# Token mixing of batches 2 to 7 written as seven block products instead of eight

## The chip, the cores and the metric

The kernel runs on one core of a Trainium2 chip. The number that counts is the device time of one execution in microseconds (us). The core has engines that run side by side, each working its own instructions strictly in order: TensorE (PE in the profile, matmuls into the PSUM banks), VectorE (DVE), ScalarE (ACT) and GpSimd (POOL). SyncE (SP) issues the transfers, also in order, on one queue. Semaphores tie the engines together, so that an instruction which waits holds up everything behind it on its own engine.

## The reference

```python
# attention: 8 batches, 8 heads, S = 576 positions, head size 64; banded masks
scores = where(mask, q @ k.T / 8, -1e9);  attn = softmax(scores);  o = attn @ v
# mixing: x is o with the heads side by side, 8 x 576 x 512
theta  = x @ w_theta
zr, zi = x * cos(theta), x * sin(theta)
y      = einsum('ts,bsd->btd', w_tok_r, zr) + einsum('ts,bsd->btd', w_tok_i, zi)
u      = x + y
out    = u + max(u @ w_ch, 0)
```

## The kernel before

All matrices are float32. For TensorE each one is split into a high and a low part (type fp32r), and a product is three matmuls: high by high, low by high, high by low. A split costs one ACT instruction (the cast that makes the high part) and one POOL or DVE instruction (the subtraction that makes the low part).

**The token stage** of a batch is the pair of einsums. The function `token` (L836) is called for d = 0 to 3 (128 columns of x) and g = 0, 1 (halves of 288 output positions). Each call sums over nine key tiles: 0 to 3 are 128 rows each of x·cos, 4 to 7 of x·sin, and tile 8 holds the last 64 rows of both. Nine tiles by three matmuls of 128x128 by 128x288 make 27 matmuls a call and 216 a batch (L850), all into one PSUM bank; `residual` (L817) then adds x to the bank on DVE (L825) and splits the sum u on ACT (L828) and POOL (L830). The weights of all 18 blocks (key tile by half) lie in SBUF the whole time: `wtk…`, `late_wt_a`, `late_wt_b`.

**Trig.** `theta` makes x·w_theta in PSUM, one key tile (st) after the other in the order 4, 0, 1, 2, 3. `trig` (L763) makes cosine and sine on ACT (K on L787, then L796, L698, L705) with a DVE step (L789), `by_x` (L745, L748) multiplies each of the two by x on DVE, and `zsplit` (L633) splits each product (ACT L644, POOL L646). Tile 4 begins with a DVE addition (g, L784).

**Attention.** For a pair of heads, `scores` (L441) runs nine small groups of matmuls into two PSUM banks, DVE masks them (L409) and takes the maximum (L498), ACT takes the exponentials (L504), DVE sums and inverts (L507, L508), and POOL multiplies (L510), which gives P. `turn` (L514) transposes P on DVE (L525, eight instructions), `pv` (L603) multiplies by v on TensorE, and x is then evacuated on ACT (L581), split (L593, L597, L599) and turned through DRAM (L729, then transfers).

**Order.** `phase(b, nb)` (L889) writes out the TensorE order by hand for a stage in which batch b is in its token and channel stages while batch nb = b + 1 is in attention and trig. Tables say behind which of the eight token calls the scores and pv of the four pairs stand: `S_AT = {2: 0, 3: 1, 4: 3, 5: 5}` puts pairs 2 and 3 of batch nb and pairs 0 and 1 of batch nb + 1 ahead of calls 0, 1, 3 and 5, `PV_AT` does the same for pv. Behind the eight token calls theta tiles alternate with the first five calls of `chan` (L869, 12 matmuls each, with `finish` on DVE, L859), and three more follow. On the other engines the framework's scheduler sets the order, once, when the program is built.

Of the kernel before, what the change touches and what calls it, by code (L numbers as in the profile page):

```python
# [38 lines left out]
FG0 = {4: ("zl2", "zl6"), 0: ("zl3", "zl7"), 1: ("zh3", "zh7")}  # L39
# [14 lines left out]
NK = 9  # L54

# [96 lines left out]
def build(ctx, tc, qT, kT, vw, wth, wtk, wch, maskb, ident, identb, outT):  # L152
# [17 lines left out]
    def pe(ins):  # L170
        tc.keep_in_program_order(ins)
# [81 lines left out]

    KE = S + 32
# [9 lines left out]
    idt = cp.tile([128, 128], F32, name="idt")  # L264
    mskb = cp.tile([128, 6, BW], BF16, name="mskb")
    idb = cp.tile([128, 128], BF16, name="idb")
# [101 lines left out]
    def token_weights(g, n, stage):  # L368
        cs = slice(HS * g, HS * g + HS)
        c = 2 * n  # L370
        src, sz = (wtk[:, c:c + 2, cs], 2 * HS) if n < 4 else (wtk[:, c, cs], HS)
        T, tag = yield from unpack(src, sz, f"wtk{g}_", stage, g == 0, n, None)
        if g:
            for p in range(NP):
                yield None, ("pv", 0, p)
            t, o = (late("wt_a", 8 * HS), 4 * HS * n) if n < 2 else (late("wt_b", 10 * HS), 4 * HS * (n - 2))
            dst = tuple(t[:, o + i * sz:o + i * sz + sz] for i in range(2))
        else:
# [254 lines left out]
    def zsplit(b, kt, z, rel):  # L633
# [3 lines left out]
        hi = hp.tile([128, DM], F32R, tag=f"zh{kt}", name=f"zh{b}_{kt}")  # L637
        lo = hp.tile([128, DM], F32R, tag=f"zl{kt}", name=f"zl{b}_{kt}")
# [123 lines left out]

    def trig(b, st):  # L763
        cs = slice(128 * st, min(128 * st + 128, S))
# [4 lines left out]
        if b == 0 and st in FG0:  # L769
            K, gt = (hp.tile([128, DM], F32R, tag=t, name=f"{n}{b}_{st}").bitcast(F32) for t, n in zip(FG0[st], "Kg"))  # L770
            K = K.bitcast(I32)[:R]
            rf = rg = None
        else:
            rf, rg = ("f", (yield from take("f", 2))), ("g", (yield from take("g", 2)))
            K = gp.tile([128, DM], I32, tag="f", name=f"K{b}_{st}")[:R]
            gt = gp.tile([128, DM], F32, tag="g", name=f"g{b}_{st}")
# [112 lines left out]
    def phase(b, nb):  # L889
        if nb >= B:  # L890
            for f, i, g in UNITS:
                go(f(b, i, g))
            return
        n = 0
        while n <= TH_AT:
            for p in S_AT:
                if S_AT[p] == n and nb + p // NP < B:
                    go(scores(nb + p // NP, p % NP))
            f, i, g = UNITS[n]
            go(f(b, i, g))  # L900
            for p in range(NP):
                if PV_AT[p] == n:
                    go(pv(nb, p))
            for p in TURN_AT:
                if TURN_AT[p] == n and nb + p // NP < B:
                    go(turn(nb + p // NP, p % NP))
            for p in range(NP):
                if PV_AT[p] == n and nb > 1:
                    x_turn(nb, p)
            if n == STORE_AT and nb > 1:  # L910
                x_store(nb)
            if n == LOAD_AT and nb > 1:
                x_load(nb)
            n += 1
        rest = UNITS[n:]
        for i, st in enumerate(STS):
            go(theta(nb, st))
            f, e, g = rest.pop(0)
            go(f(b, e, g))
            go(trig(nb, st))  # L920
            for p in TURN_TH:
                if TURN_TH[p] == i and nb + p // NP < B:
                    go(turn(nb + p // NP, p % NP))
# [135 lines left out]
```

## Time and profile before

| what | value |
|---|---|
| time, three runs | 578.02, 578.47, 578.80 us; median 578.47 us |
| span of the profiled execution | 576.0 us |
| share of the span busy: PE, DVE, ACT, POOL | 96%, 66%, 60%, 39% |
| instructions: PE, DVE, ACT, POOL | 5464, 1156, 939, 206 |
| read from and written to device memory | 64.49 MB, 16.52 MB |
| packets of the SP queue, as share of 16 engines' span | 43.7% |

The span runs from the first to the last instruction of the profiled execution on the core; the time is the whole execution as the device counts it. The stage of one batch repeats: TensorE starts the scores of pair 2 of the next batch at 273.39, 338.59 and 403.80 us. In the rows of the profile, a busy time is the sum over a group of instructions, "ns" is the mean of one, and the figure behind the bar is the time for which the engine stood idle ahead of the group, with what ended that idle time behind the arrow.

### The profile page before, as it was taken

Reading aid. Unit: us, or ns where it says so; the run is one execution under the profiler, and the core shown is the slowest. Engines: PE = TensorE matmul, PEld = TensorE weight load, DVE = VectorE, ACT = ScalarE, POOL = GpSimd, SP = SyncE. Lnnn points to the kernel's source line nnn. Section 1 sums busy time; section 2 is a strip of 40 time slices with the busy share of each in tenths; the row PEclk is TensorE's granted clock in tenths of the full one; section 3 lists DMA queues with packets and bytes.
Section 4 is the critical chain, followed back from the end, with each engine's and each line's share of the span. In section 5 each row is a group of like instructions: output and inputs, shape, how many; then the busy total and the mean of one; then the engine's idle time right before and its main releaser. Section 6 shows DMA issues by size and latency. Waiting matters only on the chain.

```text
span 576.0 us, 13996 instructions
## 1 busy us (share of the span) xinstructions
PE 550.5 (96%) x5464; PEld 501.6 (87%) x5464; DVE 378.0 (66%) x1156; ACT 345.2 (60%) x939; POOL 222.2 (39%) x206
## 2 busy tenths in 40 slices
PE   5997799999999999999999999999999999999997
PEld 4744688879999899988999899988999899989997
DVE  3879798865666668756776768756775767445112
ACT  1498967768555784369555785359556695266110
POOL 2228855525224352226324253226323353325220
PEclk9999699899999999999999999999999999999999
DMA  8991437601747046540746146550747123321002
GB/s 303 400 368 28 165 105 245 216 0 63 231 150 193 32 162 210 169 127 20 268 143 172 64 148 202 181 136 11 252 146 190 69 83 102 77 89 65 18 1 83
DMA packets 45586, 81.91 MB, mean 142 GB/s; under 512 B 3920, under 2 KB 19024, under 8 KB 45520
## 3 DMA queue, kind: packets, MB, share of 16 engines
q1 hardware_dynamic: 45520, 81.02, 43.7%
q8 instruction: 43, 0.70, 0.5%
q14 instruction: 23, 0.19, 0.1%
HBM read 64.49 MB, written 16.52 MB: 141 GB/s over the span
## 4 chain that ended last, share of the span: by engine, by line
DVE 34%; ACT 30%; PE 25%; issue 5%; POOL 2%; DMA 2%; SPq 0%; ACTq 0%; POOLq 0%; DVEq 0%
DVE pt L525 16%; PE y L850 11%; ACT P L504 11%; PE c L882 6%; PE th L685 3%; DVE P L409 3%; ACT K L698 3%; ACT K L787 3%; DVE xh L599 3%; ACT th L796 2%; ACT zh L644 2%; DVE xq L729 2%; DVE K L789 2%; ACT cos L705 2%; ACT x L581 2%
## 5 line engine op out<-in xcount | busy, mean ns | idle before, releaser
L830 POOL TENSOR_TENSOR u<-x,u 128x288 fp32r<-128x288 f32 x64 | 54.7, 858 | 184.6 <-ACT u L828 184.6
L525 DVE STREAM_TRANSPOSE pt<-P 32x288 f32<-32x288 f32 x224 | 105.1, 469 | 12.0 <-POOL P L510 8.9
L882 PE MATMUL c<-u,late_wc 128*128 128x288 f32 x768 | 110.2, 296 | 2.8 <-DVE x L859 2.8
L882 PEld LDWEIGHTS c<-u,late_wc 128*128 128x128 f32 x768 | 106.0, 188 | 6.8 <-DVE x L859 4.0
L850 PE MATMUL y<-wtkh,zh 128*128 128x288 f32 x288 | 90.3, 314 | 1.1 <-ACT zh L644 1.1
L850 PE MATMUL y<-wtkh,zl 128*128 128x288 f32 x288 | 86.2, 299 | 4.0 <-POOL zl L646 4.0
L646 POOL TENSOR_TENSOR zl<-g,zh 128x512 fp32r<-128x512 f32 x40 | 52.3, 1316 | 97.5 <-ACT zh L644 84.5
L504 ACT ACTIVATE P<-P,mx 128x64 f32<-128x64 f32 x216 | 72.0, 335 | 25.8 <-DVE mx L498 25.8
L850 PE MATMUL y<-wtkl,zh 128*128 128x288 f32 x288 | 85.9, 298 | 0.0
L828 ACT CAST u<-x 128x288 fp32r<-128x288 f32 x64 | 26.9, 429 | 86.2 <-DVE x L825 85.5
L685 PE MATMUL th<-wthh,xh 128*128 128x512 f32 x224 | 74.8, 395 | 0.3 <-DVE g L784 0.3
L850 PE MATMUL y<-late_wt_b,zh 128*128 128x288 f32 x320 | 68.1, 297 | 0.0
L825 DVE TENSOR_TENSOR x<-y,x 128x288 f32<-128x288 f32 x64 | 28.1, 448 | 53.6 <-PE y L850 53.5
L850 PEld LDWEIGHTS y<-wtkh,zl 128*128 128x128 f32 x288 | 55.1, 191 | 4.7 <-POOL zl L646 4.7
L850 PEld LDWEIGHTS y<-wtkh,zh 128*128 128x128 f32 x288 | 54.9, 191 | 4.7 <-ACT zh L644 2.3
L850 PE MATMUL y<-late_wt_a,zh 128*128 128x288 f32 x256 | 56.3, 301 | 0.0
L850 PEld LDWEIGHTS y<-wtkl,zh 128*128 128x128 f32 x288 | 55.1, 191 | 0.3 <-issue 0.3
L510 POOL TENSOR_TENSOR P<-P,sm 128x576 f32<-128x576 f32 x32 | 37.5, 1172 | 41.1 <-DVE sm L508 18.1
L850 PEld LDWEIGHTS y<-late_wt_b,zh 128*128 128x128 f32 x320 | 51.4, 189 | 0.3
L685 PEld LDWEIGHTS th<-wthh,xh 128*128 128x128 f32 x224 | 42.0, 188 | 9.2 <-DVE g L784 0.6
L850 PE MATMUL y<-late_wt_b,zl 128*128 128x288 f32 x160 | 47.4, 296 | 0.0
L581 ACT COPY x<-o 128x576 f32<-128x576 f32 x32 | 29.4, 919 | 28.4 <-PE o L617 19.1
(108 smaller groups left out, 1106.3 us busy)
## 6 DMA issues: line engine op xcount, KB each, us to landing
q<-in_qT_dram SPq DMA_DIRECT2D x32, 576.0 KB, 5.2
va<-in_vw_dram SPq DMA_DIRECT2D x30, 320.0 KB, 3.2
k<-in_kT_dram SPq DMA_DIRECT2D x28, 304.0 KB, 5.5
out_dram<-x SPq DMA_DIRECT2D x28, 288.0 KB, 2.4
vb<-in_vw_dram SPq DMA_DIRECT2D x29, 256.0 KB, 3.8
xd<-xq SPq DMA_DIRECT2D x24, 288.0 KB, 5.1
xn<-xd SPq DMA_DIRECT2D x24, 256.0 KB, 3.4
st_wtk<-in_wtk_dram SPq DMA_DIRECT2D x8, 576.0 KB, 8.8
```

The source lines that it names most:

```text
L409: pin(nc.vector.tensor_tensor_reduce(out=P[:, n], in0=ps[:, n - g0], in1=mskb[:, mask_of(pr, n)], op0=ALU.add, op1=ALU.max, scale=1.0, sca ...
L504: table(nc.scalar.activation(P[:, n], P[:, n], AF.Exp, bias=mx[:, n:n + 1], scale=SCALE, accum_out=sm[:, n:n + 1]))
L510: pin(nc.gpsimd.tensor_tensor(P, P, sm.unsqueeze(2).to_broadcast([128, NJ, BW]), op=ALU.mult))
L525: pin(nc.vector.transpose(pmats[b, pr][k0:k0 + QB, :, hh, QB * e:QB * e + QB], P[p0:p0 + QB, :, QB * o:QB * o + QB]))
L581: pin(nc.scalar.copy(dst, src))
L646: pin(nc.gpsimd.tensor_tensor(lo, z, hi.bitcast(F32), op=ALU.subtract))
L685: pe(nc.tensor.matmul(pt, l, r, start=(n == 0), stop=(n == 3 * NC - 1)))
L825: pin(nc.vector.tensor_tensor(x[:, ts], ps, x[:, ts], op=ALU.add))
L828: pin(nc.scalar.copy(uh[b, d][:, ts], x[:, ts]))
L830: pin(nc.gpsimd.tensor_tensor(ul[b, d][:, ts], x[:, ts], uh[b, d][:, ts].bitcast(F32), op=ALU.subtract))
L850: pe(nc.tensor.matmul(ps, l[:, cs], r, start=(n == 0), stop=(n == 3 * NK - 1)))
L882: pe(nc.tensor.matmul(ps, l[:, cs], r[:, ts], start=(n == 0), stop=(n == 3 * NC - 1)))
```

## The change

For batches 2 to 7 the two by two block structure (real and imaginary part by the halves g) is multiplied by Strassen's scheme. Key tiles 0 to 3 of x·cos and x·sin are combined into sums r1, i1, s1, s2, s3, s4, i2 of 128x256 pieces, the weights into sums t1 to t4, and each of the seven products is 4 tiles by 3 matmuls for each of two column blocks, 168 matmuls. Key tile 8 stays apart (`ninth`): 8 by 3 matmuls. That is 192 in place of 216 a batch. Batches 0 and 1 keep the old form.

Core of the diff, shortened:

```diff
+FIRST = 2
+S_FAST = {2: 0, 3: 1, 4: 4, 5: 8}
+PV_FAST = {0: 0, 1: 2, 2: 4, 3: 7}
+    def trig_fast(b, st):
...
+        by_x(b, st, f, cs)
...
+        nc.vector.tensor_tensor(F["i2"]..., x2, s2n, op=ALU.mult)
+        nc.scalar.copy(F["r1h"], r1)
+        nc.gpsimd.tensor_tensor(F["s1"], r2, F["i2"], op=ALU.add)
+        nc.vector.tensor_tensor(s1n, x1, s1n, op=ALU.mult)
+        eng = nc.vector if st == STS[-1] else nc.gpsimd
+        eng.tensor_tensor(F["s3"], r1, r2, op=ALU.subtract)
+        nc.scalar.copy(F["i1h"], i1)
+        nc.gpsimd.tensor_tensor(F["r1l"], r1, F["r1h"].bitcast(F32), op=ALU.subtract)
+        s2 = r2
+        nc.vector.tensor_tensor(s2, F["s1"], r1, op=ALU.subtract)
+        nc.vector.tensor_tensor(F["i1l"], i1, F["i1h"].bitcast(F32), op=ALU.subtract)
+        nc.scalar.copy(F["s2h"], s2)
+        nc.vector.tensor_tensor(F["s4"], i1, s2, op=ALU.subtract)
+        nc.gpsimd.tensor_tensor(F["s2l"], s2, F["s2h"].bitcast(F32), op=ALU.subtract)
+    def split_set(b, m, name):
...
+        for n in range(2):
+            a = slice(2 * n, 2 * n + 2)
+            nc.scalar.copy(hi[:, a], x[:, a])
+            nc.gpsimd.tensor_tensor(lo[:, a], x[:, a], hi[:, a].bitcast(F32), op=ALU.subtract)
+    def fetch(n, t):
+        nc.sync.dma_start(t.bitcast(F32), scratch(n))
+    def build_sets(j):
...
+        nc.vector.tensor_tensor(a, *W[0], op=ALU.add)
+        nc.gpsimd.tensor_tensor(c, *W[1], op=ALU.add)
...
+            nc.scalar.copy(h, x)
+            nc.gpsimd.tensor_tensor(x.bitcast(F32R), x, h.bitcast(F32), op=ALU.subtract)
+            for i, y in enumerate((h.bitcast(F32), x)):
+                nc.sync.dma_start(scratch(name)[:, HS * (4 * n + 2 * i + k):][:, :HS], y)
+    def fast_steps(b):
...
+        def s2():
+            for c in range(2):
+                products(ps["A", c], Z[1], W[1], c, (3,), False, True)
+                add("A", c, c, 0)
+            fetch("t3", wt_g)
+            split_set(b, 7, "s3")
...
+            split_set(b, 5, "s1")
+        def s3(c):
+            products(ps["A", c], Z[6], W[6], c, range(4), False, True, True)
+            u = gp.tile([128, DM], F32, tag="f", name=f"U{b}_{c}")[:, :HS]
+            nc.scalar.copy(u, ps["A", c])
+            for d, g in ((2 + c, 1), (2 + c, 0), (c, 1)):
+                x = xf[b, d][:, HS * g:HS * g + HS]
+                nc.gpsimd.tensor_tensor(x, x, u, op=ALU.add)
...
+        def s5(c):
+            open_bank("C", c, "xt"[c])
+            products(ps["C", c], Z[7], W[7], c, range(4), True, False)
+            ninth(b, ps["C", c], 2 + c, w9b, True)
+            add("C", c, 2 + c, 1)
...
     def phase(b, nb):
...
+        if b == FIRST - 1:
+            nc.sync.dma_start(scratch("b11"), wt_g.bitcast(F32))
...
+                    if BUILD_AT[j] == n:
+                        build_sets(j)
```

In the sources the four sums A, B, C, D are PSUM banks, each with two column blocks c; steps s0 to s11 (thirteen calls) stand where the eight token calls stood. `add` puts a bank onto x on DVE; U is bank A copied on ACT and added by POOL to three pieces of x. `build_sets` is called behind the first four token calls of batch 1; it makes the weight sums and stores them in device memory. From there `fetch` brings five pieces of 128x2304 (1.18 MB each) in every batch into the three places `wt_g`, `late_wt_a`, `late_wt_b`; `late_wt_b` keeps t1. The products s3, s1, i2 and s4 are split later, in the token stage, by `split_set`.

Three places in the engines' orders. The number behind a name's first letters is the batch, then the pair, the tile or the column block; the last number counts buffers. First DVE at the end of trig of batch 4 (batch 3 is in its channel stage). Before:

```order
L748 TENSOR_TENSOR g4_3_4324<-xn4_4079,th4_3_4295 128x512 [waits DMAHW4_49,Activation_49]
L859 SCALAR_TENSOR_TENSOR x3_1_2840<-c3_1_1_4340,x3_1_2840 128x288 [waits PE_49]
L748 TENSOR_TENSOR K4_3_4323<-xn4_4079,cos4_4148 128x512 [waits Activation_49]
L859 SCALAR_TENSOR_TENSOR x3_2_2910<-c3_2_1_4355,x3_2_2910 128x288 [waits PE_49]
L859 SCALAR_TENSOR_TENSOR x3_3_3052<-c3_3_1_4370,x3_3_3052 128x288 [waits PE_49]
L409 ISA P5_2_4385,mx5_2_4386<-s5_2_0_4388,mskb_93 128x64 [waits PE_49]
```

and in the changed kernel (the line numbers are those of its own source; L770 is `by_x`, L1111 is `finish`, L427 the masks, L828 to L837 lie in `trig_fast`):

```order
L828 TENSOR_TENSOR th4_3_4483<-xn4_4245,th4_3_4483 128x256 [waits DVE_49]
L770 TENSOR_TENSOR K4_3_4511<-xn4_4245,cos4_4312 128x512 [waits Activation_49]
L1111 SCALAR_TENSOR_TENSOR x3_2_3101<-c3_2_1_4545,x3_2_3101 128x288 [waits PE_49]
L835 TENSOR_TENSOR i1l_4_4363<-th4_3_4483,i1h_4_4362 128x256 [waits Activation_49]
L830 TENSOR_TENSOR s3_4_4366<-K4_3_4511 128x256 [waits DVE_49]
L834 TENSOR_TENSOR K4_3_4511<-s1_4_4367,K4_3_4511 128x256 [waits DVE_49,Pool_49]
L1111 SCALAR_TENSOR_TENSOR x3_3_3189<-c3_3_1_4560,x3_3_3189 128x288 [waits PE_49]
L837 TENSOR_TENSOR s4_4_4369<-th4_3_4483,K4_3_4511 128x256 [waits DVE_49]
L427 ISA P5_2_4575,mx5_2_4576<-s5_2_0_4578,mskb_94 128x64 [waits PE_49]
```

Behind the last product with the cosine there stood two `finish` steps; now four instructions of 128x256 stand there as well, one of them (L834) behind a POOL sum, and the theta bank is read until L837.

Second, POOL from the multiplication of pair 3 of batch 4 (P4_3) to that of pair 1 of batch 5 (P5_1), while batch 3 is in its token stage. Before (L510 is the multiplication, L830 the split of u, L597 and L599 that of x):

```order
L510 TENSOR_TENSOR P4_3_3632<-P4_3_3632,sm4_3_3634 128x576 [waits DVE_49,Activation_49,Pool_49]
L830 TENSOR_TENSOR u3_2_3779<-x3_2_2910,u3_2_3779 128x288 [waits PE_49,Activation_49,Pool_49]
L830 TENSOR_TENSOR u3_3_3890<-x3_3_3052,u3_3_3890 128x288 [waits Activation_49,Pool_49]
L830 TENSOR_TENSOR u3_0_3589<-x3_0_2720,u3_0_3589 128x288 [waits Activation_49]
L510 TENSOR_TENSOR P5_0_3813<-P5_0_3813,sm5_0_3815 128x576 [waits DVE_49,Pool_49]
```

and in the changed kernel (L528 is the multiplication, L846 `split_set`, L922 the split of u, L970 the sums with U):

```order
L528 TENSOR_TENSOR P4_3_3773<-P4_3_3773,sm4_3_3775 128x576 [waits DVE_49,Activation_49]
L922 TENSOR_TENSOR u3_0_3864<-x3_0_2824,u3_0_3864 128x288 [waits Activation_49]
L846 TENSOR_TENSOR i2l_3_4006<-i2_3_3458,i2h_3_4005 128x512 [waits Activation_49,Pool_49]
L922 TENSOR_TENSOR u3_1_3874<-x3_1_2973,u3_1_3874 128x288 [waits Activation_49]
L846 TENSOR_TENSOR i2l_3_4006<-i2_3_3458,i2h_3_4005 128x512 [waits Activation_49]
L970 TENSOR_TENSOR x3_2_3101<-x3_2_3101,U3_0_3933 128x288 [waits DMAHW1_49,Activation_49]
...
L846 TENSOR_TENSOR s4l_3_4077<-s4_3_3459,s4h_3_4076 128x512 [waits PE_49,Activation_49]
L846 TENSOR_TENSOR s4l_3_4077<-s4_3_3459,s4h_3_4076 128x512 [waits Activation_49]
L970 TENSOR_TENSOR x3_3_3189<-x3_3_3189,U3_1_3999 128x288 [waits DMAHW2_49,Activation_49]
...
L970 TENSOR_TENSOR x3_1_2973<-x3_1_2973,U3_1_3999 128x288 [waits DMAHW0_49]
L528 TENSOR_TENSOR P5_0_3938<-P5_0_3938,sm5_0_3940 128x576 [waits DVE_49,Activation_49]
```

Between the two multiplications stood three splits of u; now there are two of them, four splits of 128x512 and six sums with U (two and one of them behind the "..." lines).

Third, DVE in the first token steps of batch 3, in the changed kernel only (L543 is the transpose of P, L516 the maximum, L939 `add`), where what stood in the old order was the same transpose with one `residual` (L825) behind it:

```order
L543 STREAM_TRANSPOSE pt0_107<-P4_2_3665 32x9x32 [waits Pool_49]
L543 STREAM_TRANSPOSE pt0_107<-P4_2_3665 32x9x32 x7
L516 TENSOR_SCALAR mx4_3_3774<-mx4_3_3774 128x9 [waits DVE_49]
L939 TENSOR_TENSOR x3_0_2824<-A3_0_3714,x3_0_2824 128x288 [waits PE_49]
L939 TENSOR_TENSOR x3_1_2973<-A3_1_3724,x3_1_2973 128x288 [waits PE_49]
```

The sum with bank A stands behind the eight transposes. On TensorE (the end of bank B, then pv of pair 1, L635) the matmul that goes on accumulating in bank A waits for it:

```order
L908 MATMUL B3_1_3832<-wtkl4_629,zh3_8_3413 128x288
L908 MATMUL B3_1_3832<-wtkh4_628,zl3_8_3414 128x288
L635 MATMUL o4_1_3884<-pt1_109,va4_1_3210 64x64 [waits DMAHW2_49,Activation_49]
...
L635 MATMUL o4_1_3884<-pt1_109,vb4_1_3757 64x64 [waits DMAHW0_49]
...
L908 MATMUL A3_0_3714<-late_wt_a_787,s2h_3_3454 128x288 [waits DMAHW2_49,DVE_49]
```

The last row is new: in the old order each token call had a bank of its own, and no matmul went on in a bank that DVE had read.

More of the change, by code (lines that the diff above doesn't have):

```diff
@@ L377, in token_weights @@
             dst = tuple(t[:, o + i * sz:o + i * sz + sz] for i in range(2))
+        elif n < 2:
+            dst = tuple(wt_g[:, 4 * HS * n + i * sz:4 * HS * n + i * sz + sz] for i in range(2))
         else:
@@ L889, in phase @@
     def phase(b, nb):
[L890 to L923, printed above, removed]
+        fast = b >= FIRST
+        if fast:
+            steps = fast_steps(b)
+            at = S_FAST, PV_FAST, TURN_FAST, STORE_FAST, LOAD_FAST
+        else:
+            steps = [lambda u=u: go(u[0](b, u[1], u[2])) for u in UNITS[:8]]
+            at = S_AT, PV_AT, TURN_AT, STORE_AT, LOAD_AT
```

218 lines of the change are left out of this document (211 added, 7 removed).

## The prediction

> **What bounds the kernel now.** I read the busy shares first, then the chain of work that ended last, then the windows of single stages.
>
> ```profile
> PE 550.5 (96%) x5464; PEld 501.6 (87%) x5464; DVE 378.0 (66%) x1156; ACT 345.2 (60%) x939; POOL 222.2 (39%) x206
> ```
>
> TensorE looks like the bound, and a change that takes matmuls away looks like a gain of that size. The chain says otherwise:
>
> ```profile
> DVE 34%; ACT 30%; PE 25%; issue 5%; POOL 2%; DMA 2%; SPq 0%; ACTq 0%; POOLq 0%; DVEq 0%
> ```
>
> DVE and ACT hold 64% of it. The chain in order of time, its longest pieces, shows where:
>
> ```profile
> 338.43 0.69 DVE K L748
> ...
> 341.62 2.57 ACT P L504 x15
> ...
> 365.86 1.38 ACT P L504 x8
> ...
> 375.52 3.10 ACT P L504 x18
> ...
> 379.78 1.16 POOL P L510
> 384.85 0.69 DVE g L784
> ...
> 403.64 0.69 DVE K L748
> 404.33 0.73 DVE x L859 x2
> ```
>
> From one end of trig (338.43) to the next (403.64) it is masks, exponentials, multiplication, transposes, then the trig of five tiles: a round of DVE, ACT and POOL that feeds itself and takes 65.2 us a batch with TensorE nowhere in it. TensorE runs just under that round:
>
> ```profile
> core 0: us, PE busy (x) PEld busy (x) DVE busy (x) ACT busy (x) POOL busy (x), PEclk, DMA share, GB/s
> 143.00:208.20 65.20, 64.68 (x659) 60.66 (x658) 44.44 (x157) 40.62 (x120) 23.72 (x23) 1.00 0.48 142
> 338.59:403.80 65.21, 64.65 (x658) 60.64 (x657) 45.36 (x159) 41.10 (x121) 24.27 (x23) 1.00 0.49 148
> 531.20:576.00 44.80, 41.49 (x314) 41.26 (x312) 7.77 (x17) 3.47 (x8) 6.86 (x9) 1.00 0.11 40
> ```
>
> It is busy for 64.65 of 65.21 us at clock 1.00. So there are two limits at almost one height, and the change lowers one and loads the other. Only the last batch, 44.8 us, is TensorE's alone.
>
> **TensorE.** The price of a matmul is in the last batch, which waits for nothing:
>
> ```profile
> 531.36 28.62 PE y L850 x216
> ```
>
> 28.62 / 216 = 0.1325 us. A batch loses 24 matmuls, 3.18 us; six batches 19.1 us. That is the most the change can bring. The stage could shrink to 65.2 - 3.2 = 62.0 us.
>
> **What the other engines get.** Prices of the shapes:
>
> ```profile
> L646 POOL TENSOR_TENSOR zl<-g,zh 128x512 fp32r<-128x512 f32 x40 | 52.3, 1316 | 97.5 <-ACT zh L644 84.5
> L830 POOL TENSOR_TENSOR u<-x,u 128x288 fp32r<-128x288 f32 x64 | 54.7, 858 | 184.6 <-ACT u L828 184.6
> L644 ACT CAST zh<-g 128x512 fp32r<-128x512 f32 x35 | 21.2, 605 | 0.1
> L828 ACT CAST u<-x 128x288 fp32r<-128x288 f32 x64 | 26.9, 429 | 86.2 <-DVE x L825 85.5
> L748 DVE TENSOR_TENSOR K<-xn,cos 128x512 f32<-128x512 f32 x24 | 16.5, 687 | 16.2 <-ACT cos L705 16.2
> L825 DVE TENSOR_TENSOR x<-y,x 128x288 f32<-128x288 f32 x64 | 28.1, 448 | 53.6 <-PE y L850 53.5
> ```
>
> Pieces of 128x256 are not in this trace. On the line through 288 and 512 elements they cost 0.41 us on DVE, 0.40 on ACT and 0.79 on POOL; the 288 rows bound that from above, and half of the 512 rows (0.34, 0.30, 0.66) from below. I take the line, as it lies next to the 288 row.
>
> DVE: out go 4 products with the sine (4 x 0.69); in come 4 x 5 pieces and s3 of the last tile (21 x 0.41), and 4 more sums of 288 (4 x 0.45): +7.6 us, 45.4 to 53. ACT: out go 8 casts of 512; in come 12 of 256, 8 of 512 in the token stage and 2 copies of U: +12 x 0.40 + 2 x 0.43 = +5.7, 41.1 to 46.8. POOL: out go 8 splits of 512; in come 15 pieces of 256 (15 x 0.79), 8 splits of 512 and 6 sums with U (6 x 0.86): +17.0, 24.3 to 41.3. Each stays under 62, so no engine becomes the bound by its sum. What counts is where the pieces stand in the round.
>
> **The round, in two pieces.** I cut it at the addition g of tile 4 (384.85 + 0.68) and at the first mask (339.8, one round on 405.0): 45.7 us of attention and 19.5 us of trig.
>
> Trig. In the old kernel the tail behind the last K (400.27 on ACT, to 404.33) is the sine, the cosine, two products. The order now puts i1l, s3, s2 and s4 of that tile behind the last `by_x`, with a POOL sum between: 4 x 0.41 + 0.79, about 2.5 us more, and the second score group waits for s4, which reads the theta bank last. DVE in this piece was busy for 13.5 us (8 finishes at a pitch of 0.38, and 5 K steps and 10 products at about 0.69); it now has 8.6 more and 2.8 less, 19.4 us, so its waits for ACT at the front no longer hide behind slack. With 2.7 us of such waits (the sine of tile 4 and its product) the piece takes 19.4 + 2.7 = 22.1. I take **+2.7**; bounds are 0 (everything in the old waits) and +5.8 (everything on top).
>
> Attention. Here the order helps and hurts. Helps: the adds of bank D and the transposes of pair 0 stand beside the exponentials of pair 1 (375.52, 3.10 us) instead of ahead of its maximum:
>
> ```profile
> 371.38 3.85 DVE L525 STREAM_TRANSPOSE pt<-P 32x288 f32<-32x288 f32 x8
> 375.26 0.17 DVE L498 TENSOR_SCALAR mx<-mx 128x9 f32<-128x9 f32 x1
> ```
>
> That can be worth 3.9 us. Hurts: POOL now has four splits and six sums between two multiplications that stood 22 us apart; 6 x 1.32 (with s3 and s1) and 6 x 0.86 make the sum with C of column 1, and the multiplication of pair 0 behind it, about 1.2 us late, and the multiplication of pair 1 stands behind a split of u, 0.9 us. Walking the order through with these durations I get 43.2 to 43.8 for this piece; bounds are 41.8 (the full 3.9 gained) and 46.5. I take 43.8, **-1.9**, as some delay by contention is sure to come (below).
>
> The round: 65.2 + 2.7 - 1.9 = **66.0 us**, bounds 62.0 (TensorE) and 68.5. TensorE waits out the difference, mainly in two places of the order: the second score group, which waits for s4, and the third step, which waits for the sum with A behind eight transposes (3.86 us).
>
> **Contention.** The same DVE subtraction took twice as long beside POOL:
>
> ```profile
> 347.14 0.68 DVE L599 TENSOR_TENSOR xh<-x,xh 128x512 fp32r<-128x512 f32 x1
> ...
> 356.86 1.65 DVE L599 TENSOR_TENSOR xh<-x,xh 128x512 fp32r<-128x512 f32 x1
> ```
>
> ```profile
> 356.75 1.21 POOL L510 TENSOR_TENSOR P<-P,sm 128x576 f32<-128x576 f32 x1 [2.67 <-ACT xh L593]
> ```
>
> The second began 0.1 us behind a POOL instruction and lasted until 0.55 us after its end. Both of its inputs lie in SBUF. Of the new DVE pieces only s2 (4 a batch) and s3 are of this kind; the others read PSUM. [...]
>
> [...] I took 0.6 us of it in the 43.8 and price the rest as a rival.
>
> **Once, at the start.** Batch 1 builds the weight sums: 4 x 5 + 3 DVE steps of 288 (10 us), 28 + 1 on POOL (25 us), 17 on ACT (7 us) and 34 transfers, between 143 and 208 us, where DVE was busy for 44.4 and POOL for 23.7 us. They fit by sum, but they stand in order among the multiplications and masks, and the loads of x for trig stand behind stores that wait for POOL. One group between a mask and its multiplication is 3 x 0.86 on POOL and 2 x 0.45 on DVE. I take +1.8 us for the attention piece, between 0 and 6, and +2.7 for trig, which has the new form from here: **+4.5**.
>
> **The sum**, against the span of 576.0 us: start +4.5; four rounds (batches 2 to 5) +0.8 each, +3.2; the slack of 0.5 us by which TensorE trailed the round, -0.5; batch 6, with half the attention, -3.2 from TensorE and +2.7 from trig, -0.5; batch 7 -3.2 and +1.0 for its third step and its split products, -2.2. Together +4.5, 580.5. The median of the runs, 578.5, is 2.5 over the span: **583 us**.
>
> **Rivals.** *The short round.* Steps that follow each other without a wait cost less than their own duration:
>
> ```profile
> 404.24 0.82 DVE L859 SCALAR_TENSOR_TENSOR x<-c,x 128x288 f32<-128x288 f32 x2
> 391.74 2.55 POOL L646 TENSOR_TENSOR zl<-g,zh 128x512 fp32r<-128x512 f32 x2 [9.27 <-ACT zh L644]
> ```
>
> Two in 0.82 and in 2.55 us, against 2 x 0.45 and 2 x 1.32. If the 21 pieces in trig run at 0.34 instead of 0.41, that piece loses 1.5 us, POOL's twelve steps 0.7, and the round is 63.5 to 64: four rounds -6, batch 6 -2, batch 7 -2.2, slack -0.5, start +4.5: -6, **572 us**. If it falls to TensorE's 62.0: four rounds and batch 6 -16, **564**. The gain starts where the round is under 65 us, 1.0 under my forecast. For it: the old chain's waits for ACT leave room. Against: nearly all new pieces depend on each other. This is the side on which I am wrong if I am.
>
> *The long round.* With 2 us more of contention a batch the round is 68: five times 2 more, **592**. [...]
>
> *Weights late.* The sets t3, b22 and b11 share one place, so t3 is asked for only when A has used b11. A load of 576 KB takes 5.2 us here, 1.18 MB about 3 at the 400 GB/s of the start and 7 at the 170 GB/s of a busy slice:
>
> ```profile
> GB/s 303 400 368 28 165 105 245 216 0 63 231 150 193 32 162 210 169 127 20 268 143 172 64 148 202 181 136 11 252 146 190 69 83 102 77 89 65 18 1 83
> q<-in_qT_dram SPq DMA_DIRECT2D x32, 576.0 KB, 5.2
> ```
>
> Between the request and the first use lie 60 to 70 matmuls, 8 to 9 us (less in batch 7). One late set a batch, by 1 us: 583 + 6, **589**.
>
> **How the numbers follow.** Forecast 0.46 (577 to 588), short round 0.36 (564 to 577), long round 0.12, late weights 0.06. A measurement tells about 0.2% from no change: faster means under 577.3, slower over 579.6. All of the short round is faster; of the forecast's range 0.10 of chance lies within, 0.02 below: faster 0.38, same 0.10, slower 0.52. For 8 in 10 the range goes from 567 (0.09 below) to 592 (0.07 above).
>
> **What would show it.** Right: a period of about 66 us between the scores of pair 2, the last piece of trig some 2.5 us behind its `by_x`, TensorE idle for 3 to 4 us a batch ahead of the second score group and of the third step, and the first new batch 4 to 5 us late. Short round: the chain goes through PE, and the period is 62 to 64. Late weights: PE waits for the fetch ahead of bank C or D. Wrong altogether: the clock under 1.00 in the waits, or the builds holding batch 1 by over 9 us.

## The result and the profile after

The changed kernel takes 606.11 us (median of 4 runs, 603.35 to 609.01), the kernel before 578.25 us beside it: 1.049 times as long, 95% interval 1.044 to 1.054. Slower, as forecast, but by 28 us and not by 4.5. The profile is that of the slowest of these four runs (609.01 us), so its parts add up to some 3 us more than the median.

Part 1 of the page of the changed kernel, busy time, share of the span and instructions:

```profile
PE 546.3 (90%) x5320; PEld 492.6 (81%) x5320; DVE 450.9 (74%) x1305; ACT 381.5 (63%) x1040; POOL 341.8 (56%) x361
```

TensorE has 144 matmuls fewer and still only 4 us less busy time, though 144 x 0.1325 is 19 us. The windows of three stages of equal build (the table load of the exponential to the next) tell a part of the reason:

```profile
core 0: us, PE busy (x) PEld busy (x) DVE busy (x) ACT busy (x) POOL busy (x), PEclk, DMA share, GB/s
226.00:296.00 70.00, 63.78 (x632) 59.12 (x632) 55.02 (x180) 46.47 (x135) 40.08 (x45) 0.98 0.66 222
296.00:366.00 70.00, 64.09 (x632) 59.26 (x632) 55.39 (x182) 46.89 (x136) 40.20 (x45) 0.98 0.66 222
366.00:434.00 68.00, 62.29 (x632) 57.74 (x632) 54.80 (x182) 46.31 (x135) 40.02 (x45) 1.00 0.69 228
```

At full clock TensorE is busy for 62.3 us, 2.4 us less than the 64.65 before, where 3.18 were worked out; in the two stages at clock 0.98 it is busy for 63.8 and 64.1 us. Up to the end of trig of batch 2 it was busy for 194.6 us against 189.4 before, with no more matmuls to do; from 121.24 us on the clock there was 0.98 and then 0.85, and 1.00 in the same stretches before. The sums on the other engines came out within 1.8 us (DVE 54.8, ACT 46.3, POOL 40.0, against 53, 46.8 and 41.3). But the stage is 68 us long, 5.7 us of them with TensorE idle, and in two of the stages the granted clock is below 1.

To put the time in its places, ACT's two table loads mark each stage: one ahead of the first sine of trig (L796 before, L806 now), one ahead of the first exponential behind it (L504, L522). Timeline rows of ACT, start and length, before:

```profile
209.38 1.28 ACT L504 ACT_TABLE_LOAD   x1
...
386.22 1.28 ACT L796 ACT_TABLE_LOAD   x1
405.00 1.28 ACT L504 ACT_TABLE_LOAD   x1
```

and in the changed kernel:

```profile
226.82 1.28 ACT L522 ACT_TABLE_LOAD   x1
...
273.93 1.28 ACT L806 ACT_TABLE_LOAD   x1
296.29 1.28 ACT L522 ACT_TABLE_LOAD   x1
...
365.73 1.28 ACT L522 ACT_TABLE_LOAD   x1
...
411.30 1.28 ACT L806 ACT_TABLE_LOAD   x1
433.68 1.28 ACT L522 ACT_TABLE_LOAD   x1
```

Trig, from the first load to the second, went from 18.8 to 22.4 us; attention from 46.4 (339.79 to 386.22) to 45.6 us; a round from 65.2 to 67.95. That is a stage at full clock; in the two at 0.98 trig took the same 22.4 us, attention 47.1 and the round 69.4 us. (The forecast cut the round at two DVE steps, which gives 45.7 and 19.5 us before; only the differences are compared.) Over the whole execution (span 607.2 against 576.0):

| stretch | before | after | difference | forecast |
|---|---|---|---|---|
| to the end of trig of batch 2 (209.38, 226.82) | 209.4 | 226.8 | +17.4 | +4.5 |
| four rounds, batches 2 to 5 | 260.8 | 274.8 | +14.0 | +2.7 |
| batches 6 and 7 | 105.8 | 105.6 | -0.2 | -2.7 |

The four rounds took 69.5, 69.4, 68.0 and 68.0 us.

Where TensorE waits, from its timeline in three stages (the bracket is its idle time and what ended it):

```profile
296.68 0.82 PE L486 MATMUL s<-k,q 128*64 128x64 f32 x16 [2.14 <-DVE s L837]
...
366.12 0.69 PE L486 MATMUL s<-k,q 128*64 128x64 f32 x16 [2.14 <-DVE s L837]
378.63 0.53 PE L908 MATMUL A<-late_wt_a,s2h 128*128 128x288 f32 x2 [0.83 <-DVE x L939]
393.57 0.69 PE L635 MATMUL o<-pt,vb 128*64 128x64 f32 x16 [2.40 <-DMA vb<-in_vw_dram]
```

Two of these places were named ahead of the run: the second score group behind s4 and the third step behind the sum with A. That for v was not.

### The profile page after: what moved, and what is told of

It is laid out like the page before. It is cut to its first block, busy times and chain, and to the rows that moved or that the text cites. A ratio compares the mean times of both kernels' runs of the same rounds, so it can differ in the third digit from the quotient of the medians.

```text
span 607.2 us, 14364 instructions
## 1 busy us (share of the span) xinstructions
PE 546.3 (90%) x5320; PEld 492.6 (81%) x5320; DVE 450.9 (74%) x1305; ACT 381.5 (63%) x1040; POOL 341.8 (56%) x361
## 4 chain that ended last, share of the span: by engine, by line
DVE 41%; PE 18%; ACT 18%; DMA 10%; issue 6%; POOL 6%; SPq 1%; POOLq 0%; DVEq 0%; ACTq 0%
DVE pt L543 14%; ACT P L522 5%; PE c L1134 4%; PE A L908 3%; DVE P L427 3%; DVE xh L617 3%; DMA st_wtk<-in_wtk_dram 2%; DVE K L770 2%; DMA va<-in_vw_dram 2%; PE C L908 2%; PE th L707 2%; DVE xq L751 2%; DMA tw_t<-tb 2%; DVE x L939 2%; DVE K L834 2%
## 5 line engine op out<-in xcount | busy, mean ns | idle before, releaser
L543 DVE STREAM_TRANSPOSE pt<-P 32x288 f32<-32x288 f32 x224 | 105.0, 469 | 10.0 <-POOL P L528 7.0
L522 ACT ACTIVATE P<-P,mx 128x64 f32<-128x64 f32 x216 | 72.0, 335 | 23.0 <-DVE mx L516 23.0
L528 POOL TENSOR_TENSOR P<-P,sm 128x576 f32<-128x576 f32 x32 | 37.4, 1168 | 58.2 <-DVE sm L526 33.9
L707 PEld LDWEIGHTS th<-wthh,xh 128*128 128x128 f32 x224 | 43.1, 192 | 22.7 <-issue 6.2
L922 POOL TENSOR_TENSOR u<-x,u 128x288 fp32r<-128x288 f32 x48 | 38.2, 806 | 32.6 <-ACT u L921 32.6
L486 PE MATMUL s<-k,q 128*64 128x64 f32 x1008 | 40.1, 234 | 10.3 <-DVE s L837 8.6
L486 PEld LDWEIGHTS s<-k,q 128*64 128x64 f32 x1008 | 35.5, 147 | 15.1 <-ACT s2h L836 9.0
L707 PE MATMUL th<-wthl,xh 128*128 128x512 f32 x112 | 44.6, 398 | 0.0
L522 ACT ACTIVATION_READ_ACCUMULATOR P<-P,mx 128x1 f32 x216 | 40.4, 187 | 0.0
L427 DVE CUSTOM_DVE_ANT_0 P<-s,mskb 128x64 f32<-128x64 f32 x216 | 34.6, 213 | 5.3 <-PE s L486 5.3
L1111 DVE SCALAR_TENSOR_TENSOR x<-c,x 128x288 f32<-128x288 f32 x64 | 28.7, 448 | 10.8 <-PE c L1134 10.7
L668 POOL TENSOR_TENSOR zl<-g,zh 128x512 fp32r<-128x512 f32 x7 | 9.1, 1294 | 42.5 <-ACT zh L666 42.5
L599 ACT COPY x<-o 128x576 f32<-128x576 f32 x32 | 29.4, 920 | 4.0 <-PE o L635 4.0
L970 POOL TENSOR_TENSOR x<-x,U 128x288 f32<-128x288 f32 x36 | 30.6, 878 | 0.0
L838 POOL TENSOR_TENSOR s2l<-K,s2h 128x256 fp32r<-128x256 f32 x24 | 17.6, 735 | 20.8 <-ACT s2h L836 20.8
L846 POOL TENSOR_TENSOR s3l<-s,s3h 128x512 fp32r<-128x512 f32 x12 | 15.2, 1287 | 23.6 <-ACT s3h L845 23.6
L635 PE MATMUL o<-pt,vb 128*64 128x64 f32 x464 | 19.3, 226 | 9.0 <-DMA vb<-in_vw_dram 9.0
## 6 DMA issues: line engine op xcount, KB each, us to landing
q<-in_qT_dram SPq DMA_DIRECT2D x32, 576.0 KB, 4.8
```

Source lines behind the costliest of these rows:

```text
L427: pin(nc.vector.tensor_tensor_reduce(out=P[:, n], in0=ps[:, n - g0], in1=mskb[:, mask_of(pr, n)], op0=ALU.add, op1=ALU.max, scale=1.0, sca ...
L486: pe(nc.tensor.matmul(ps[64 * e:64 * e + 64, n - g0], q[:, qb], k[:, QB * qb:QB * qb + BW], start=not masked, stop=not masked or n == g1 - 1))
L522: table(nc.scalar.activation(P[:, n], P[:, n], AF.Exp, bias=mx[:, n:n + 1], scale=SCALE, accum_out=sm[:, n:n + 1]))
L528: pin(nc.gpsimd.tensor_tensor(P, P, sm.unsqueeze(2).to_broadcast([128, NJ, BW]), op=ALU.mult))
L543: pin(nc.vector.transpose(pmats[b, pr][k0:k0 + QB, :, hh, QB * e:QB * e + QB], P[p0:p0 + QB, :, QB * o:QB * o + QB]))
L599: pin(nc.scalar.copy(dst, src))
```

## The experiments

The marks of ACT give for every run the shortest round of batches 3 to 5 (sine to sine), its attention and its trig, and the start (sine of batch 1 to sine of batch 2). All in us, from one profiled execution of each, but for the time, which is the median of the runs:

| run | time | start | round | attention | trig |
|---|---|---|---|---|---|
| before | 578.3 | 69.7 | 65.2 | 46.4 | 18.8 |
| changed | 606.1 | 83.1 | 67.95 | 45.6 | 22.4 |
| e1 old, 24 matmuls fewer | 564.4 | 69.7 | 63.0 | 43.9 | 19.1 |
| e2 no loads | 602.4 | 81.6 | 67.95 | 45.6 | 22.4 |
| e3 and no stores | 596.5 | 77.7 | 68.0 | 45.6 | 22.4 |
| e4 and no sums | 590.1 | 72.0 | 68.0 | 45.6 | 22.4 |
| e5 s2 with one SBUF input | 604.7 | 82.6 | 67.7 | 45.9 | 21.8 |
| e9 GpSimd only writes | 600.7 | 82.3 | 68.0 | 45.5 | 22.5 |
| e7 U on VectorE | 623.2 | 82.8 | 71.3 | 47.3 | 24.0 |
| e8 other bank | 602.0 | 82.1 | 67.9 | 45.9 | 22.0 |
| e10 builds apart | 605.7 | 79.9 | 67.95 | 45.6 | 22.4 |
| e11 no U sums | 614.4 | 82.8 | 69.6 | 47.1 | 22.6 |
| e12 less on VectorE | 610.8 | 81.9 | 69.6 | 46.1 | 23.5 |
| e13 both | 626.1 | 82.6 | 70.1 | 46.7 | 23.4 |
| e17 order | 606.0 | 83.4 | 67.3 | 45.5 | 21.8 |
| e18 order, bank | 595.1 | 82.2 | 66.0 | 44.2 | 21.8 |
| e19 VectorE twice | 619.0 | 81.8 | 68.4 | 45.5 | 22.9 |
| e20 GpSimd twice | 655.1 | 83.1 | 75.0 | 52.3 | 22.7 |
| e22 order, bank, no U | 594.8 | 83.5 | 66.1 | 43.7 | 22.4 |
| e23 order, bank, free start | 583.6 | 72.0 | 66.0 | 44.2 | 21.8 |

Two things limit what the table can say. The changed kernel and the thirteen runs whose edit does not touch the start read 81.6 to 83.5 us there, so a difference of 2 us in the start is scatter. And the scheduler lays its orders anew for every edit. In a steady round VectorE's instructions stand in the changed kernel's order in e2, e3, e4 and e10, and in e23 in that of e18. In e5, e7, e8, e9, e11, e12, e13, e19 and e20 the order differs from the changed kernel's, in e22 from e18's. Those runs change work and order together, and give no price of the work alone.

**Is the old round VectorE's and ScalarE's alone?** (in `token`)

```diff
-        for kt in KORD:
+        for kt in KORD[:8 if b >= 2 else NK]:
...
```

> The kernel before, with key tile 8 left out of the token sums of batches 2 to 7 (24 matmuls a batch fewer, nothing else; the output lacks that tile). Round theory (the chain of VectorE, ScalarE and GpSimd sets 65.2 us a batch): the period of batches 2 to 5 stays at 64.7 to 65.2 us, only batch 7 and a part of batch 6 get shorter by 3.2 us each; time 570 to 575 us. Rival (TensorE sets the period): six times 3.18 us less, period 62.0 us, time about 559 us.

564.36 us, ratio 0.976 [0.974, 0.978]: between the two. The round shrank to 63.0 us, nearer to the 62.0 of TensorE. The chain without TensorE, on which the forecast was built, was a tie: with less work on TensorE the scheduler laid another order for VectorE, and the round shrank with it. In the old order the transposes of pair 2 stood ahead of the last masks and the maximum of pair 3, in this one behind the masks (DVE rows from 346.30 to 352.58 us before, from 342.38 to 348.28 us in e1):

```
before:  masks 1-6 of P4_3, transposes of P4_2, masks 7-9, maximum of P4_3
e1:      masks 1-9 of P4_3, transposes of P4_2, maximum of P4_3
```

So a kernel that gives TensorE 24 matmuls less for nothing gains 14 us, and the changed kernel has to explain 42 us, not 28.

**The start and the loads.** e2 leaves out the five loads a batch, e3 the stores of the sums and of two blocks of the weights as well, e4 the sums too:

```diff
 def fetch(n, t):
-        nc.sync.dma_start(t.bitcast(F32), scratch(n))
+        (e2: for the first t1 and t2 only; e3, e4: nothing)
 def build_sets(j):
...
-                nc.sync.dma_start(scratch(name)...[:, :HS], y)
+                (e3: nothing)
 def phase(b, nb):
...
-            nc.sync.dma_start(scratch("b11"), wt_g.bitcast(F32))
-            nc.sync.dma_start(scratch("b22"), ...)
+            (e3, e4: nothing)
...
-                        build_sets(j)
+                        (e4: nothing)
```

> The changed kernel, with the five loads of weight sums a batch left out (t1 and t2 are loaded once, the places hold old weights, so the output is another). Round and contention theory: the waits of TensorE for v (0.9 to 2.4 us a batch) go, but the chain does not pass through them; time 600 to 606 us, period still 67 to 68 us. Rival (streamed weights and their traffic hold the stage up): period 65 to 66 us, time 590 to 595 us.

> As the run without loads, and the weight sums of batch 1 are made but not stored, with no load of t1 and t2 either (output another). If the start is lost to waits for stores (buffers of the sums come free only when their stores have landed): the stage of batch 1, 81.4 us in the changed kernel, falls to 70 to 72 us, time 10 us under the run without loads. If it is lost to the 69 instructions themselves: it stays at 78 us or more.

> As the run without stores, and the four groups of weight sums are not made at all (the ninth tile's sum stays; output another). Stage of batch 1: 65.2 us plus the longer trig (3.9 us in the later stages), so 68 to 70 us by both theories; the difference to the run without stores is the price of the instructions: 1 to 3 us by the store theory, 9 us or more by the instruction theory.

602.4, 596.5 and 590.1 us. The loads do not hold the round (67.95 with and without): TensorE's wait for v went, and one of 1.2 us for the sum with C came up in its place. What e2 gained lies at the end. Batches 6 and 7 take 105.6 us in the changed kernel and 105.4 in e10, but 101.4 to 101.7 in e2, e3 and e4. So the loads cost some 4 us there; through which wait is not shown.

The start falls in steps: 83.1, 81.6, 77.7, 72.0 and 69.7 before. The first step is scatter, for in the changed kernel no load of the weight sums is issued before the stretch ends at 204.31 us. The first one, in the queue:

```profile
205.42 0.32 SPq L861 DMA_DIRECT2D late_wt_b<-tw_t  x1
```

So, measured from starts of 81.6 to 83.5, the stores cost 4 to 6 us of the 13.4, the sums themselves 5.7, and 2.3 remain without both. In e4's trace the ninth tile's sum (`build_ninth`) stands in that place. Its cast on ACT waits for VectorE, and the table load of the exponential stands behind it:

```profile
145.78 0.43 ACT L896 CAST t<-t_sum 128x288 fp32r<-128x288 f32 x1 [4.09 <-DVE mx L516]
146.23 1.28 ACT L522 ACT_TABLE_LOAD   x1
```

The first exponential comes 28.1 us behind the sine's table load of batch 1 there, and came 24.6 us behind it before. To the +17.4 of the table above trig of batch 2, in its new form, adds 3.7. Neither theory was right alone: the one on stores expected 70 to 72 us in e3, the one on instructions 78 or more and then 9 us for the sums. Both parts show in the chain of the changed kernel, a store's landing ahead of the next group and again ahead of trig's first step on ACT:

```profile
156.34 5.98 DMA tw_t<-tb
...
162.44 1.07 POOL ta L872
...
197.75 4.55 DMA tw_t<-tb
...
202.40 0.07 ACT tb L881
...
202.73 0.62 ACT K L804
```

The casts `tb` (L881) wait until the store that still reads their buffer has landed; K of trig (L804) stands behind them in ACT's order. With the groups moved apart,

```diff
-BUILD_AT = {0: 0, 1: 1, 2: 2, 3: 3}
+BUILD_AT = {0: 0, 1: 2, 2: 4, 3: 6}
```

> The changed kernel with the four groups of weight sums behind token calls 0, 2, 4 and 6 of batch 1 instead of 0 to 3 (same result). If the start is lost because groups wait for each other's stores and crowd between masks and multiplications: the stretch from the sine's table load of batch 1 to that of batch 2, 83.1 us in the changed kernel and 69.7 before, falls to 76 to 79 us, time 600 to 602 us. Rival (the instructions delay VectorE and the x loads wherever they stand): it stays at 82 to 85 us, time 605 to 608 us.

605.7 us, start 79.9: 1.7 us under the least of the untouched starts, less than the 76 to 79 expected, and lost in the scatter of the time (604.96 to 606.41).

**Contention, the tail, and the amount of work.** Four edits of the changed kernel:

```diff
 e5:
-        nc.vector.tensor_tensor(s2, F["s1"], r1, op=ALU.subtract)
+        nc.vector.tensor_tensor(s2, i1, r1, op=ALU.subtract)
 e9: (and s2l; s3 of the first three tiles)
-        nc.gpsimd.tensor_tensor(F["r1l"], r1, F["r1h"].bitcast(F32), op=ALU.subtract)
+        nc.gpsimd.memset(F["r1l"].bitcast(F32), 0.0)
 e7:
...
-            nc.scalar.copy(u, ps["A", c])
...
-                nc.gpsimd.tensor_tensor(x, x, u, op=ALU.add)
+                add("A", c, d, g)
 e8:
-TP = {4: "t", 0: "s", 1: "s", 2: "t", 3: "s"}
+TP = {4: "t", 0: "s", 1: "s", 2: "t", 3: "x"}
-        return "mmx"[n % 3] if b else "m"
+        return ("mmm" if n >= 8 and b >= 1 else "mmx")[n % 3] if b else "m"
```

> The changed kernel with s2 made from the theta bank and r1 instead of s1 and r1 (one input in SBUF instead of two; the wait for GpSimd stays, the output is another). Contention theory: the four s2 of a batch take 0.41 us instead of 0.56 to 0.95, trig (table load of the sine to that of the exponential, 22.4 us) falls to 21.2 to 21.6, period 67.9 to 67.0, time 600 to 602 us. Rival (the number of VectorE pieces and their dependences): under 0.3 us a batch, time 604 to 606 us.

> The changed kernel in which 11 of the 15 GpSimd pieces of trig a batch (r1l, s2l and the first three s3) are replaced by writes of zero to the same places, which read nothing (the output is another). Contention theory: trig falls from 22.4 to 21.2 us or less, as in the run with s2 from the theta bank, time 600 us or less. Rival (VectorE's own pieces bound trig): trig stays at 22 us or more, time 603 to 606 us.

> The changed kernel with U added to its three pieces by VectorE straight from bank A (6 sums of 288 on VectorE more, 6 on GpSimd and 2 copies on ScalarE fewer; the same result). If GpSimd's queue and its contention lengthen attention (45.6 us against 44.2 us in the old kernel with 24 matmuls fewer): it falls to 44 us, time 599 to 602 us. Rival (VectorE's sum of work bounds attention): 6 x 0.37 = 2.2 us more, 47 us or more, time 612 us or more.

> The changed kernel with theta of key tile 3 in bank x and the channel sums in bank m alone, so that the second score group no longer waits for s4 (the same result). Tail theory: TensorE's wait of 2.1 us a batch goes, and the masks come 0.9 us earlier: period 67.9 to 67.0 us, time 601 to 603 us. Rival (the first exponentials are held by VectorE's queue, not by the bank): no change, 605 to 607 us.

In e5 an s2 takes 0.42 us in the mean instead of 0.78, which is 1.5 us a batch; trig got 0.55 us shorter (21.8 for 22.4) and the round 0.25 us. In e9, where 11 of GpSimd's 15 pieces read nothing, s2 takes 0.42 us too, and trig stays at 22.5. So contention on s2 is not what made trig 3.6 us longer; 0.55 us is the most that shows. With U on VectorE the round is 71.3 us, as its rival said; how much of that is the work and how much the other order and the clock (0.93 to 0.98 in its rounds, 0.967 over the execution) was not separated. The other bank removes the 2.1 us wait, and a wait of the same length comes up at the next place, the sum with A. Timeline of TensorE in that run:

```profile
305.62 0.69 PE L908 MATMUL A<-late_wt_a,s2h 128*128 128x288 f32 x2 [2.06 <-DVE x L939]
```

Taking work away altogether:

```diff
 e11: (both also in e13)
-            for d, g in ((2 + c, 1), (2 + c, 0), (c, 1)):
...
-                nc.gpsimd.tensor_tensor(x, x, u, op=ALU.add)
 e12: (s4 likewise)
-        nc.vector.tensor_tensor(F["i1l"], i1, F["i1h"].bitcast(F32), op=ALU.subtract)
+        nc.gpsimd.memset(F["i1l"].bitcast(F32), 0.0)
```

> The changed kernel without the six sums with U on GpSimd (their copies on ScalarE stay; output another). GpSimd theory for attention: it falls from 45.6 us to 44 us, the 44.2 us of the old kernel with 24 matmuls fewer; time 598 to 600 us. Rival (VectorE's own work in attention): 45 us or more, time 602 us or more.

> The changed kernel with i1l and s4 (8 of the 21 VectorE pieces of trig a batch) written as zeros by GpSimd instead (output another). VectorE theory: 8 x 0.37 = 3.0 us less on VectorE, trig from 22.4 to 19.5 us, period from 67.9 to 65 us, time 592 to 594 us. Rival (trig is held by ScalarE and by dependences): trig at 21.5 us or more, time 601 us or more.

> The last two edits together (output another). If trig and attention are two separate debts, their gains add: period 63.5 to 64 us, which is near the 63.0 us of the old kernel with 24 matmuls fewer, time 585 to 588 us. Rival (a third limit, weights or the matmul clock): period 66 us or more, time 595 us or more.

All three are slower: 614.4, 610.8, 626.1 us. The theories of the gains all missed. Their rivals hold by their numbers, which were open upwards, but none foresaw that less work takes more time. The scheduler laid another order for VectorE in all three, and that this order costs more than the work saves is the likely reading; it was not singled out. What the trace shows is longer waits: without the U sums TensorE waited up to 2.51 us at the second score group and up to 3.25 us for v, and the clock was 0.62 from 366 to 370 us and 0.71 from 396 to 400 us, the windows in which these two end. Timeline of TensorE:

```profile
367.18 1.12 PE L486 MATMUL s<-k,q 128*64 128x64 f32 x16 [2.51 <-DVE mx L427]
...
396.86 0.69 PE L635 MATMUL o<-pt,vb 128*64 128x64 f32 x16 [3.25 <-DMA vb<-in_vw_dram]
```

**Order or work.** e17 ties the transposes, which stay together, behind the next pair's maximum (and those of pair 2 behind the sums with A), and calls two of the `turn`s two steps later; e18 has the other bank as well:

```diff
-TURN_FAST = {2: 0, 3: 2, 4: 8}
+TURN_FAST = {2: 2, 3: 4, 4: 8}
...
+    def after(ins, earlier):
+        for e in earlier:
+            tc.add_manual_dep(ins.ins, e.ins.name,
...
 def turn(b, pr):
...
+            if b > FIRST and i == 0 or pr < 2 and b > FIRST + 1 and i == 0:
+                first = [mxs[b * NP + pr + 1]] if b * NP + pr + 1 in mxs else []
+                if pr == 2:
+                    first += adds.get((b - 1, "A"), [])
+                after(t, first)
+            if i and b > FIRST:
+                after(t, [last])
```

e19 makes i1l and s4 twice on VectorE, e20 each low part of the split products twice on GpSimd (`for _ in range(2):` ahead of the instruction).

> The changed kernel with one thing about VectorE's order laid down for batches 3 on: the eight transposes of a pair stand behind the maximum of the next pair, and those of pair 2 behind the two sums with A as well (same work, same result). Order theory (what holds the round at 68 us is where the transposes stand, not how much work there is): exponentials of pairs 3 and 0 start 3.8 us earlier, TensorE's wait for the sum with A (0.8 us) goes, attention falls from 45.6 us to 43 us or less, period to 65.5 us or less, time 592 to 596 us. Rival (the work itself): period 67 us or more, time 602 us or more.

> The same order and theta of key tile 3 in bank x (same result). The bank alone moved TensorE's wait to the sum with A, which the order takes away: order theory period 64 to 65 us, clock 1.00 in the windows, time 585 to 591 us. Rival (the work itself): 600 us or more.

> The changed kernel with i1l and s4 made twice (8 more VectorE pieces a batch, 3.0 us; same result). If VectorE's work is the bound: period 67.9 to 70.5 us or more, time 618 to 622 us. If order and waits are: under 1 us a batch, time 606 to 612 us.

> The changed kernel with the eight low parts of the split products made twice (8 more GpSimd steps of 512 a batch, 10.2 us in attention; same result). If GpSimd's queue sets attention: period plus 5 us or more, time 630 us or more. If it has room: under 2 us a batch, time 606 to 616 us.

606.0, 595.1 (ratio to the kernel before 1.032 [1.029, 1.034]), 619.0 and 655.1 us. The order alone brought 0.6 us a round at best, none of it in attention (45.5), and no time. TensorE's wait for the sum with A went, the one at the second score group was 2.5 us, and two of the four rounds had a clock of 0.95 and 0.98 (0.969 over the execution). With the bank as well the round falls to 66.0 us, the clock is 1.00 in all four rounds, and attention is 44.2 to 44.6 us, near e1's 43.9. So order and bank together bring 1.4 us of attention at best; neither does alone (45.5 and 45.9).

The two runs with more work tell less than they seem to. Eight more steps of 128x256 on VectorE lengthened two of the four rounds by 4.1 and 4.7 us and changed the others by -1.0 and +0.4 us; the clock over the execution was 0.972, against 0.969 in the changed kernel. 9.5 us more on GpSimd lengthened each round by 5.6 to 7.1 us, and the place is in sight: once a round TensorE waits 5.1 to 6.3 us for the low part of i2, and the clock of the rounds is 0.91 to 0.93 (0.937 over the execution). Timeline of TensorE in e20:

```profile
412.40 0.61 PE L909 MATMUL C<-late_wt_a,i2l 128*128 128x288 f32 x1 [5.14 <-POOL i2l L847]
```

This shows that GpSimd has no room for that much more, and not that it is a limit as the changed kernel stands. Last, with that order:

```diff
 e22: e18 without the six sums with U
 e23: e18 without fetch, build_sets and the two stores of the weight blocks
```

> The run with the laid down order and the other bank, without the six sums with U on GpSimd (output another). GpSimd theory (its 22 us without a gap in the second half of attention are the limit now): 5.2 us less there, period from 66.0 to 63 or 64 us, time 581 to 587 us. Rival (VectorE or the order): period 65.5 us or more, time 592 us or more.

> The run with the laid down order and the other bank, without the weight sums of batch 1, their stores and all loads of them (output another): what the scheme would cost if its weights were there for nothing. Start theory: the stretch between the sine's loads of batches 1 and 2 falls from 82.2 to 71 or 72 us, the rounds stay at 66 us, time 580 to 584 us, no better than the kernel before. Rival (the rounds themselves are lengthened by the loads): period 64.5 us or less, time 575 us or less.

594.8 and 583.6 us (1.012 [1.009, 1.015]). With 5.0 us less on GpSimd attention is 0.5 us shorter and trig 0.5 us longer, in another order of VectorE's; nothing in it says that GpSimd is the single limit. e23 keeps e18's order. With the weights for nothing the scheme is still no faster than the old kernel, 1.2% slower: its round is 66.0 us, where e1 has 63.0, and 2.7 of the 3 us lie in trig (21.8 against 19.1).

## Why the prediction was right in sign and wrong in size

The sign came as forecast, at a chance of 0.52 for slower, little more than even. The prediction named the short round as the side on which it would be wrong; it was wrong on the other.

- **TensorE, 3.18 us a batch:** 2.4 us of busy time at full clock. "a round of DVE, ACT and POOL that feeds itself and takes 65.2 us a batch with TensorE nowhere in it" was wrong as a law: e1 shortened that round by 2.2 us with work taken from TensorE alone, and VectorE's order changed with it. The chain showed a tie, with 0.56 us of idle time on TensorE, and an order that was laid for it.
- **Sums on the other engines:** right within 1.8 us each. Pieces of 256 cost 0.41 to 0.42 us on DVE, but s2 0.78 in the mean and s3 of the last tile 0.53, both with both inputs in SBUF; on POOL they cost 0.74 to 0.78.
- **Trig +2.7:** +3.6 measured. Against e1 it is still +2.8 in e18. Trig is 21.8 us in e5, e17 and e18, by three different edits, so what part of the 3.6 us is contention and what part is order was not separated. Nor was it singled out what holds the remaining chain of ACT, DVE and POOL in trig: e5, e9 and e12 each took one link away, and trig moved by -0.55, +0.1 and +1.1 us.
- **Attention -1.9:** -0.8 to -0.9 in the two rounds at full clock, +0.7 in the two at 0.98, -1.9 to -2.2 with e18's order and bank. The gain was there, and the order and the bank that the changed kernel has did not let it through. Of the 11.3 us by which the four rounds went over the forecast this is the largest part, 7.2 us; trig has 3.5, the slack 0.5.
- **Contention, 0.6 us a round in the forecast:** too little in attention. It was the author's estimate, and no run shows it as a term, nor the 2 us more of the long round. What the runs showed in its place is 0.55 us of trig at most (e5) and rows of attention like these. Timeline rows of DVE, and of POOL beside them:

```profile
387.40 0.82 DVE L516 TENSOR_SCALAR mx<-mx 128x9 f32<-128x9 f32 x1
388.14 0.90 DVE L615 TENSOR_TENSOR xh<-x,xh 128x64 fp32r<-128x64 f32 x1
388.96 1.30 DVE L617 TENSOR_TENSOR xh<-x,xh 128x512 fp32r<-128x512 f32 x1
...
391.40 1.76 DVE L617 TENSOR_TENSOR xh<-x,xh 128x512 fp32r<-128x512 f32 x1
```

```profile
387.39 2.32 POOL L970 TENSOR_TENSOR x<-x,U 128x288 f32<-128x288 f32 x3
389.67 2.95 POOL L846 TENSOR_TENSOR s4l<-s,s4h 128x512 fp32r<-128x512 f32 x2
```

  In the kernel before, free of POOL, the same steps take 0.17, 0.22 and 0.68 us, so these four rows alone are 3.0 us longer than that. How much of these 3.0 us the round would get back was not isolated. (The POOL order shown with the change ends at the multiplication of pair 0 of batch 5, P5_0, and not of pair 1; the count of splits and sums in it is right.)
- **The slack of 0.5 and batches 6 and 7, -2.7:** the slack did not come, and the two batches brought -0.2. Attention of batch 7 took 1.1 us more (39.4 to 40.6 us) and what follows it 1.3 less (66.3 to 65.0). Without the loads the two batches are 4.1 to 4.4 us shorter than before (e2, e3, e4), so the gain is there and the loads took it.
- **The start, +4.5:** the step that failed most, 17.4. It was made of +1.8 for the stretch from sine to sine, where 13.4 were measured, and +2.7 for trig of batch 2, where 3.7 were. The 69 instructions were counted and taken to fit beside the others. The runs showed 5.7 us for the sums, 4 to 6 for their stores, since here buffers came free only when a store had landed (5.98 and 4.55 us in the chain above) and ACT's casts for them stood ahead of trig, and 2.3 that stay with the ninth tile's sum. How much late x has in it was not measured.
- **The clock:** the two rounds at clock 0.98 took 1.5 us more each than those at 1.00, 3 us in all. Of the signs named under "wrong altogether" both came: this one, and the builds holding batch 1 by over 9 us.
- **Late weights:** not in the rounds, where v came late behind the weights in the queue, at no cost by itself (e2: the round is 67.95 us without that wait). In the last two batches the loads cost some 4 us, where the rival expected about 1 us a batch.

By the profile the start is 12.9 us over its forecast, the four rounds 11.3 and the last two batches 2.5. The median lies 23 us over the forecast, and 14 us over the upper end of the range.

## What to carry to other kernels

A chain that does not pass through an engine shows what ended last in one execution, not that this engine is free: TensorE was idle for 0.56 us a round here and both could be limits, and an experiment that takes work from one (e1, 2.2 us a round) says more than the chain. When a scheduler lays the order, look first whether a run with less or more work still has the same order; e2, e3, e4, e10 and e23 did, and the others price work and order together. Work moved from a saturated engine to two others must be placed in their order, not only summed, and less work came here with another order and more time (e11, e12 and e13, 4.7 to 20.0 us). A one-time cost that reuses buffers waited here for stores to land (4 to 6 us); work it out as a chain too.

## What the runs showed of the hardware

TensorE's granted clock fell behind some waits of about 2 us and not behind others. The same 2.14 us wait ahead of the second score group was followed by these 4 us:

```profile
core 0: us, PE busy (x) PEld busy (x) DVE busy (x) ACT busy (x) POOL busy (x), PEclk, DMA share, GB/s
296.70:300.70 4.00, 4.00 (x30) 3.88 (x31) 1.39 (x17) 3.12 (x15) 0.38 (x1) 0.57 0.74 233
366.20:370.20 4.00, 4.00 (x64) 3.77 (x66) 1.33 (x17) 3.26 (x16) 0.32 (x1) 1.00 0.76 258
```

Clock 0.57 in one stage, 1.00 in the next, and the first of the two rounds 1.5 us longer. In e8 the clock was 0.60, 0.57 and 0.57 in 306 to 310, 374 to 378 and 442 to 446 us, and in the 4 us ahead of each of these TensorE was idle for 2.06, 2.05 and 2.02 us. What decides whether the clock falls was not shown. In the old kernel, whose longest wait in the stages of batches 2 to 5 is 0.58 us, the clock of these stages was 1.00.

The maximum (L516), a step on nine values a row with one input, took 0.82 us at 387.40 us beside GpSimd's sums with U, and 0.17 us in the kernel before (375.26 us) with no instruction of GpSimd beside it. Why was not shown.
